# Batch 0 of a Longformer-attention and ResMLP kernel: the shifted V by compute engines, and a new order of batch 0's work

## The chip, the cores and the metric

The kernel runs on one core of a Trainium2 chip. The metric is device time in microseconds (us) of one execution. Engine names: PE is TensorE, PEld its weight loads, DVE VectorE, ACT ScalarE, POOL GpSimd, SP SyncE. "SPq" and the like are the engines' instruction queues, from which they issue transfers (DMAs).

## The reference

Eight batches of windowed attention with eight global tokens, followed by a residual MLP block that mixes tokens and then channels. Cut to what matters (B = 8, H = 8, S = 576, D = 64; the MLP width is 512, hidden 2048):

```
scores = scale * q @ k.T
mask = |i - j| <= 32, or i global, or j global
attn = softmax(where(mask, scores, -1e9))
x = (attn @ v), heads side by side: [B, S, 512]
a1 = alpha1 * x + beta1
u = x + lam * einsum('ts,bsd->btd', w_tok, a1)
a2 = alpha2 * u + beta2
out = u + lam * (relu(a2 @ w_ch1) @ w_ch2)
```

The eight global indices are data; the kernel reads them and gathers their K and Q rows.

## The kernel before

Attention is worked in 128-row tiles for pairs of heads (hp = 0..3, two heads a of 64 columns in 128 partitions). For a batch b, K and Q are transposed to KT and QP (in batch 0, Q0). Scores come by strips of 64 queries t against 128 keys, their exponentials go to E (ACT), the band mask is multiplied in to give PT (DVE, `probs_k`), and PGQ takes the part of the global keys (`probs_q`). The global queries' rows are scored by `gk0_mm`, exponentiated into EG and, with GM, become G (`g_rows`). `gq_mm` multiplies PGQ by V; its result goes to RG in a high part (`gq_hi`, ACT) and a low part (`gq_lo`, DVE). `pv_tiles` then adds up G with RG, PT with Ve and PT with Vo for five row tiles. Ve holds V in tiles of 128 rows that begin 32 rows early; Vo holds the same rows half a tile further down: its partitions 0 to 63 are partitions 64 to 127 of Ve's tile, and its partitions 64 to 127 are partitions 0 to 63 of Ve's next tile. After a normalisation (`norm_x` for tiles 0 to 2, `norm_y` or `norm_ya` for 3 and 4) comes the product with alpha1*lam (`scale_x`, `scale_y`, in LA1) into XL and XL4, which feed the token mixing with wtT.

The MLP of 4 row tiles at a time (`mlp`, nine groups g) is the large part: 64 matmuls of 128x512 with W1, whose results leave three PSUM banks through a ReLU on ACT to HT, and 64 with W2. While group g runs, the attention of batch g+1 is woven between its matmuls at fixed places (`weave`, `timed`). Batch 0 has no MLP to lie beside. Its work is written out by hand: FIRST is a list of words, each a function in `ops`, recorded in that order; each engine executes its own instructions in the order in which they were recorded. `name:b` gives a word PSUM bank b, and `sp:n` records n spare matmuls of 256 columns (`spare`), whose results nobody uses. The last words, W1s and after, begin the MLP of group 0 and the casts of batch 1.

The words that the text below uses, for hp = h: `ck`, `cq` cast K and Q to bf16; `tk`, `tq` transpose them on PE; `kt`, `qv` bring them from PSUM to KT and Q0; `gath`, `gx`, `gt`, `ge0`, `gte`, `ge1` gather and place the global columns; `ct`, `tt`, `ktt`, `qtt` do rows 512 to 575; `z` and `s` compute scores and `e` their exponentials; `V` and `u` load V of batch 0 and 1; `pg`, `pt` are the probabilities; `q`, `ra`, `rd` the global product and its two parts; `pvx`, `nx`, `xl` and `pvy`, `nr`, `ny`, `xm` the PV product, normalisation and scaling; `wt`, `we` transpose w_tok; `rs`, `re` its row sums; `la`, `lb`, `lc` spread alpha1*lam over LA1; `tm`, `ad`, `tx`, `ut` mix tokens, add, transpose and write UT, the MLP's input; `ab`, `abe` give the bias and scale columns of `ut`; `kc`, `qc` cast K and Q of batch 1. `beta` is the row b0_beta on POOL.

`ld_const` (word gat1) issues on SP the four transfers that fill Vo in batch 0, then K and Q of batch 1 and two broadcast rows. C16 is an index ramp of 576 f16 numbers, loaded from memory (L727) and used by `gm`. `fill_pt` puts zeros in the four PT buffers, `ve_fill` zeros and ones in Ve. CK, QV, QC and NY say, per hp, which engine does a step (A, D, P for ACT, DVE, POOL).

Of the kernel before, what the change touches and what calls it, by code (L numbers as in the profile page):

```python
# [9 lines left out]
FP32 = mybir.dt.float32  # L10
FP16 = mybir.dt.float16
# [5 lines left out]
P = 128  # L17
S = 576
D = 64
H = 8  # L20
HP = 4
# [22 lines left out]
]  # L44
FIRST = """
kgz vez ktz pgz gb1 gbm:0 W0 gbc ar0 ar1 gath ck0 ar2 pgc tk0:1 sp:3 cq0 kt0 ck1 tq0:2 V0 cq1 qv0 tk1:3 mask
V1 tq1:4 sp:6 kt1 qv1 ck2 V2 idn tk2:5 sp:2 cq2 V3 kt2 gx tq2:6 V4 ck3 qv2 gt:0 ge0 tk3:1 sp:3 gte wki ge1 kt3
cq3 gat1 wi z00:2 z20:3 s20:4 s00:5 e200 ct tq3:6 e000 GM z10:0 s10:1 tt:3 sp:7 e201 ptz e101 ktt qtt e001 qv3
ab:2 z21:4 z01:1 s01:3 fz e100 s21:5 gk0:6 e011 la e010 gk1:0 abe e210 pg0 z30:3 s30:1 e211 pt0 ptz2 z11:2
s11:4 eg0 q0:5 eg1 pg2 lb:6 b1t e110 G ra0 q2:0 e111 z31:2 sp:3 rd0 e300 pg1 s31:4 beta pvx0:5 pt1 e310 e311  # L50
q1:3 sp:2 e301 nx0 ra1 pvy0:2 qz0 wt0:4 ra2 rd1 rd2 lc wt4:1 pt2 wt3:5 we0 xl0 wt2:3 we3 nr0 ny0 pvy1:0 qz1
we2 wt1:6 nr1 pg3 pvx2:4 we1 pt3 xm0 q3:5 we4 nx2 pvy2:2 pvx1:3 ra3 v1f ny1 rd3 rs:6 nr2 ny2 xl2 xm1 pvy3:1 re
pvx3:4 xm2 nx1 tm0:5 xl1 u0 nx3 tm1:6 u1 ad0 u2 xl3 tx0:3 ad1 u3 tm2:4 ut0 nr3 ny3 u4 xm3 tx1:5 ad2 b1i tm3:6
ut1 gc1 tx2:3 ad3 ut2 tx3:4 ut3 W1s qc0 kc0 qc1 kc1 qc2 kc3 qc3 kc2
"""
PLACE = {t: (g, j) for g, ts in enumerate(GROUPS) for j, t in enumerate(ts)}


def _consts():
    p = np.arange(P)  # L60
    c16 = np.zeros((P, S), np.float16)
    c16[:, :] = np.arange(S)[None, :]
    d = p[:, None] - np.arange(64)[None, :]
    band = ((d >= 0) & (d <= 64)).astype(np.float16)
    eye = np.where(np.eye(P, dtype=bool), 0x3F80, 0).astype(np.uint16)
    ab = (p % 16) // 8
    oh = ((p >= 64) & (p < 80)) | ((p >= 96) & (p < 112))
    c32 = np.zeros((P, 144), np.float32)
    c32[:, 0:9] = 64 * np.arange(9)[None, :] - 32 + p[:, None]
    c32[:, 9:18] = (c32[:, 0:9] >= 0) & (c32[:, 0:9] < S)  # L70
    c32[:, 18:26] = p[:, None] % 8 == np.arange(8)[None, :]
    b2, h = p // 64, (p % 64) // 8
    for pr in range(4):
        c32[:, 26 + pr] = ((2 * pr + b2) * H + h) * S
    for a in range(2):
        c32[:, 30 + a] = h % 2 == a
        c32[:, 32 + a] = np.where(oh & (ab == a), GSC, 0.0)
        c32[:, 34 + a] = np.where((p < 64) & (ab == a), 1.0, np.where(p == 80, EPS_A, 0.0))
    c32[:, 36] = np.where(p < 64, 1.0, 1.0 / GSC)
    c32.view(np.uint16)[:, 96:224] = eye  # L80
    c32.view(np.uint16)[:, 224:288] = band.view(np.uint16)
    return c16, c32


def weave(mlp, parts):
# [15 lines left out]
def kernel(ctx, tc, q, k, v, global_idx, alpha1, beta1, w_tok, alpha2, beta2, w_ch1, w_ch2, lam, out):  # L101
    nc = tc.nc
# [8 lines left out]
    def T(name, shape, dt):  # L111
        return cp.tile(list(shape), dt, name=name)
# [14 lines left out]
    def mm(o, l, r, st, sp):  # L127
        nc.tensor.matmul(out=o, lhsT=l, rhs=r, start=st, stop=sp, skip_group_check=True)  # L128

    c16n, c32n = _consts()  # L130
    TSB = T("TSB", [P, DM], BF16)
    C16 = T("C16", c16n.shape, FP16)
    C32 = T("C32", c32n.shape, FP32)
    identb = C32[:, 48:112].bitcast(BF16)
    band = C32[:, 112:144].bitcast(FP16)
# [9 lines left out]
    Ve = [t.rearrange("p (c h e) -> p c h e", c=5, h=H) for t in Vef]  # L145
    Vo = [T(f"Vo{i}", [P, 4, H, 65], FP16) for i in range(2)]
# [5 lines left out]
    G = T("G", [P, 2, 704], FP16)  # L152
    GM = T("GM", [P, 2, S], FP16)
# [14 lines left out]
    mask = T("mask", [P, NW, 64], FP16)  # L168
# [3 lines left out]
    A2 = T("A2", [P, DM], FP32)  # L172
# [33 lines left out]
    TST = SR[:, 1, :]  # L206
# [221 lines left out]
        nc.vector.tensor_tensor(out=xo, in0=pv[:, :, :, 0:64], in1=rb, op=ALU.mult)  # L428

    def xl_eng(b, hp):  # L430
        return nc.vector if (b, hp) in ((0, 1), (0, 3)) else nc.gpsimd

    def pv_tiles(ps, b, hp, i0, i1):
        for i in range(i0, i1):
# [173 lines left out]
    def fill(ap, val=0.0, eng=None):  # L608
        (eng or nc.vector).memset(ap, val)
# [4 lines left out]
    def ld_kq(src, st_, eng, b, h0, h1):  # L614
        eng.dma_start(
            out=st_[:, h0:h1, :, :].rearrange("p h j d -> p h (j d)"), in_=src[b, h0:h1, 0:512, :].rearrange("h (p j) d -> p h (j d)", j=4)
        )
# [4 lines left out]
    def cast_q(b, hp, copy):  # L622
        copy(out=QB0[b][:, :, 128 * hp : 128 * hp + 128].rearrange("p j (a d) -> p a j d", a=2), in_=QST[:, 2 * hp : 2 * hp + 2, :, :])
# [95 lines left out]
    nc.sync.dma_start(out=gbi[0:1, :], in_=gi32.unsqueeze(0))  # L719
    nc.scalar.dma_start(out=C32[:, 0:48], in_=c32d[:, 0:48])  # L720
    nc.scalar.dma_start(out=C32[:, 48:144], in_=c32d[:, 48:144])
    for hp in range(HP):
        ld_kq(k, KST, nc.sync, 0, 2 * hp, 2 * hp + 2)
        ld_kq(q, QST, nc.scalar if hp < 2 else nc.sync, 0, 2 * hp, 2 * hp + 2)
    ld_tail(k, TST, nc.sync, 0, 0)
    ld_tail(q, TST, nc.sync, 0, 64)
    nc.sync.dma_start(out=C16, in_=nc.inline_tensor(c16n, name="c16_np").ap())  # L727
    nc.sync.dma_start(out=LA1[0:1, :], in_=alpha1.unsqueeze(0))
    for r in (0, 64):
        nc.sync.dma_start(out=LR[r : r + 1, :], in_=lam.unsqueeze(0))  # L730
# [21 lines left out]
    def ld_w2(blk):  # L752
        g_.dma_start(out=W2[:, 8 * blk : 8 * blk + 8, :], in_=w_ch2[1024 * blk : 1024 * blk + 1024, :].rearrange("(c p) e -> p c e", p=P))

    def fill_pt(i):
        z = PT0[i][:, 0, 0:64].bitcast(FP32)
        fill(bass.AP(z.tensor, z.offset, [z.ap[0], [608, 2], [64, 10], [1, 32]]), 0.0, g_)

    def pg_zero():
        for hp in range(HP):  # L760
# [3 lines left out]
    def ve_fill(i, eng=g_):  # L764
        fill(VF[i][0:32, 0:260], 0.0, eng)
        fill(VF[i][96:128, 1040:1300], 0.0, eng)
        fill(Ve[i][:, :, :, 64:65], 1.0, eng)
# [141 lines left out]
    def ab_ev(ps):  # L909
# [5 lines left out]
    mlp0 = mlp(0)  # L915
    hb = {}
    CPY = {"A": nc.scalar.copy, "D": nc.vector.tensor_copy, "P": nc.gpsimd.tensor_copy}
    CK, QV, KC, QC, NY = "ADAD", "ADAD", "AAAA", "DDDD", "DADD"
    ops = {
        "idn": lambda: nc.scalar.copy(out=ident, in_=identb),  # L920
        "kgz": kz_fill,
        "qz1": lambda: qzero(1, g_),
        "W0": warm,
        "ct": lambda: V_.tensor_copy(out=TSB, in_=TST),
        "gc1": lambda: gcols(1),
        "ktz": lambda: kt_fill(0, V_),
        "qz0": lambda: qzero(0, g_),
        "pgz": pg_zero,
        "vez": lambda: ve_fill(0, g_),
        "ptz": lambda: (fill_pt(0), fill_pt(1)),  # L930
        "ptz2": lambda: (fill_pt(2), fill_pt(3)),
        "gat1": ld_const,
        "wki": ld_wt,
        "wi": ld_w,
# [37 lines left out]
    for h in range(HP):  # L972
        ops.update(
            {
                f"ck{h}": lambda h=h: cast_k(h, CPY[CK[h]]),
                f"cq{h}": lambda h=h: cast_q(0, h, V_.tensor_copy),
                f"tk{h}": lambda ps, h=h: pair_tr(ps, KB0, h),
                f"tq{h}": lambda ps, h=h: pair_tr(ps, QB0[0], h),
                f"kt{h}": lambda h=h: pair_k(hb[f"tk{h}"], 0, h),
                f"qv{h}": lambda h=h: pair_q0(hb[f"tq{h}"], h, CPY[QV[h]]),  # L980
                f"V{h}": lambda h=h: load_v(0, h),
                f"u{h}": lambda h=h: load_v(1, h),
                f"kc{h}": lambda h=h: cast_k(h, CPY[KC[h]]),
                f"qc{h}": lambda h=h: cast_q(1, h, CPY[QC[h]]),
                f"pg{h}": lambda h=h: probs_q(0, h),
                f"pt{h}": lambda h=h: probs_k(0, h),
                f"q{h}": lambda ps, h=h: gq_mm(ps, 0, h),
                f"ra{h}": lambda h=h: gq_hi(hb[f"q{h}"], h),
                f"rd{h}": lambda h=h: gq_lo(hb[f"q{h}"], h),
                f"pvx{h}": lambda ps, h=h: pv_tiles(ps, 0, h, 0, 3),  # L990
                f"nx{h}": lambda h=h: norm_x(hb[f"pvx{h}"], 0, h),
                f"nr{h}": lambda h=h: hb.update({f"rt{h}": recip(hb[f"pvy{h}"], 2)}) if NY[h] == "A" else None,
                f"xl{h}": lambda h=h: scale_x(0, h),
                f"pvy{h}": lambda ps, h=h: pv_tiles(ps, 0, h, 3, 5),
                f"ny{h}": lambda h=h: norm_ya(hb[f"pvy{h}"], hb[f"rt{h}"], h) if NY[h] == "A" else norm_y(hb[f"pvy{h}"], 0, h),
                f"xm{h}": lambda h=h: scale_y(0, h),
                f"tm{h}": lambda ps, h=h: tok_mm(ps, h),
                f"ad{h}": lambda h=h: tok_add(hb[f"tm{h}"], h),
                f"tx{h}": lambda ps, h=h: tok_tr(ps, h),
                f"ut{h}": lambda h=h: tok_ev(hb[f"tx{h}"], h),  # L1000
            }
        )
# [142 lines left out]
```

## Time and profile before

| | |
|---|---|
| median of 9 runs | 394.21 us (392.98 to 396.75) |
| the profiled execution: time, span | 395.14 us, 393.4 us |
| PE, DVE, ACT, POOL busy | 96%, 58%, 43%, 53% of the span |
| transfers | 48.56 MB, mean 123 GB/s |
| first MLP matmul (W1s) | 43.82 us |
| first score matmul of batch 0 | 14.13 us |
| first PV matmul, and the one that waited for Vo | 23.27 us, 26.66 us |
| first ReLU of group 0 | 48.61 us |

The span runs from the first to the last instruction; the time has 1.74 us more around it. A line of the chain or of an engine's instructions gives start, duration and what it was (engine, source line, output<-input, shape, count), and in brackets how long the engine had been idle and for what. A line of the stretches gives, for each engine, busy time and number of instructions, then the granted clock of PE, the share of the transfer engines and GB/s. The busy shares of the page are means over the whole span, most of which is the MLP stream; what happens to batch 0 has to be read in the first 50 us.

### The profile page before, as it was taken

The page shows a single profiled execution, that of the slowest core. Times are in us where ns is not written, and L with a number is a line of the kernel's source. Part 1 is how long each engine was busy: PE and PEld are TensorE (multiplying, and loading weights), DVE is VectorE, ACT ScalarE, POOL GpSimd, SP SyncE. Part 2 cuts the span into 40 slices and gives each one's busy share as a digit, 9 for nine tenths or more (in the row PEclk, how much of TensorE's full clock was granted, in tenths as well). Part 3 has the DMA queues.
Part 4 walks back from the last instruction along what each step waited for, and adds up shares of the span by engine and source line. Part 5 has one row for each costly group of instructions (what it writes and reads, how often), then busy time and mean ns, then how long its engine had stood idle before and what let it go on. Part 6 is the DMA issues. An engine that isn't in the chain of part 4 may idle for free.

```text
span 393.4 us, 8133 instructions
## 1 busy us (share of the span) xinstructions
PE 376.0 (96%) x3062; PEld 213.0 (54%) x3115; DVE 228.8 (58%) x590; ACT 169.9 (43%) x335; POOL 209.1 (53%) x273
## 2 busy tenths in 40 slices
PE   6969899999999999999999999999999999999995
PEld 2649666645654566446645664466446644444443
DVE  5868765876548555954596459645774554114023
ACT  5544787005740584038503850187018700731720
POOL 8929819559748954885377836873251245000000
PEclk9977999999999999999999999999999999999999
DMA  7999999969999995999977998899240013101002
GB/s 239 184 236 292 162 215 150 127 149 124 159 147 147 142 153 122 104 122 168 151 77 153 129 147 103 130 168 129 78 108 27 2 55 80 41 20 61 28 27 81
DMA packets 161299, 48.56 MB, mean 123 GB/s; under 512 B 147615, under 2 KB 154727, under 8 KB 161260
## 3 DMA queue, kind: packets, MB, share of 16 engines
q0 software_dynamic: 98288, 17.05, 63.8%
q1 hardware_dynamic: 62140, 30.39, 37.7%
q10 hardware_dynamic: 832, 0.60, 0.5%
q8 instruction: 24, 0.39, 0.4%
q14 instruction: 15, 0.12, 0.1%
HBM read 39.05 MB, written 9.44 MB: 123 GB/s over the span
## 4 chain that ended last, share of the span: by engine, by line
PE 85%; DMA 6%; DVE 3%; POOL 3%; issue 1%; ACT 0%; DVEq 0%
PE bank L128 84%; DMA Ve<-in_v_dram 3%; DMA Vo<-Ve 2%; POOL Ve L222 2%; DVE XR L582 1%; DVE QP L644 1%; PE bank L869 1%; POOL KQG L254 1%; DVE OT L581 1%; PE bank L634 0%; POOL UB L507 0%; DMA gbi<-in_global_idx_dram 0%; DVE XR L428 0%; POOL XL L446 0%; DVE QP L238 0%
## 5 line engine op out<-in xcount | busy, mean ns | idle before, releaser
L128 PE MATMUL bank<-UT,W 128*128 128x512 bf16 x546 | 152.6, 379 | 1.1
L128 PE MATMUL bank<-W,HT 128*128 128x512 bf16 (+2 forms) x573 | 137.3, 373 | 0.9 <-issue 0.2
L566 ACT ACTIVATE HT<-bank,bias 128x512 bf16<-128x512 f32 x128 | 87.9, 687 | 52.3 <-PE bank L128 51.5
L367 ACT ACTIVATE E<-bank 128x416 f16<-128x416 f32 (+1 forms) x84 | 42.1, 520 | 116.3 <-PE bank L128 115.5
L128 PEld LDWEIGHTS <-HT 128*128 128x128 bf16 (+1 forms) x610 | 55.1, 99 | 53.9 <-issue 1.6
L446 POOL TENSOR_TENSOR XL<-XR,LA 128x384 bf16<-128x384 f32 x30 | 30.3, 1011 | 79.6 <-DVE XR L428 49.2
L128 PEld LDWEIGHTS <-W 128*128 128x128 bf16 (+1 forms) x658 | 51.4, 97 | 25.5
L581 DVE TENSOR_TENSOR OT<-bank,LAM 128x512 f32<-128x512 f32 (+2 forms) x37 | 24.9, 673 | 55.2 <-PE bank L128 55.1
L507 POOL TENSOR_TENSOR UB<-XR,A 128x512 bf16<-128x512 f32 x28 | 35.9, 1290 | 22.5 <-DVE XR L502 15.1
L128 PE MATMUL bank<-RG,G 128*128 128x65 f16 x320 | 45.0, 197 | 0.3
L128 PE MATMUL bank<-Ve,PT 128*128 128x65 f16 x300 | 42.5, 197 | 0.0
L128 PEld LDWEIGHTS <-PT 128*128 128x128 f16 x540 | 32.0, 99 | 17.7 <-DMA Vo<-Ve 1.0
L128 PE MATMUL bank<-XL,wtT 128*128 128x512 bf16 (+2 forms) x237 | 41.0, 326 | 0.1
L128 PEld LDWEIGHTS <-G 128*128 128x128 f16 x320 | 31.8, 100 | 16.8 <-issue 1.8
L128 PE MATMUL bank<-Vo,PT 128*128 128x65 f16 x240 | 34.3, 194 | 2.8 <-DMA Vo<-Ve 2.8
L222 POOL DMA_DIRECT2D Ve<-in_v_dram x40 | 34.4, 882 | 0.2
L128 PEld LDWEIGHTS <-KT 128*128 128x128 bf16 (+1 forms) x324 | 23.2, 100 | 18.0 <-issue 1.4
L215 POOL DMA_DIRECT2D Kb<-in_k_dram x30 | 27.2, 907 | 5.0 <-DMA W<-in_moe_w_ch_dram 4.9
L128 PE MATMUL bank<-QP,KT 128*128 128x144 bf16 (+1 forms) x252 | 28.7, 223 | 0.4
L215 POOL DMA_DIRECT2D Qb<-in_q_dram x30 | 27.1, 904 | 3.6 <-DMA W<-in_moe_w_ch_dram 3.6
L428 DVE TENSOR_TENSOR XR<-bank,rd 128x384 f32<-128x384 f32 (+1 forms) x63 | 26.9, 426 | 2.4 <-DVE rd L421 0.3
L128 PEld LDWEIGHTS <-wtT 128*128 128x128 bf16 (+1 forms) x240 | 18.7, 99 | 17.4 <-issue 1.7
(153 smaller groups left out, 416.0 us busy)
## 6 DMA issues: line engine op xcount, KB each, us to landing
out_dram<-XR SPq DMA_DIRECT2D x31, 256.0 KB, 4.1
W<-in_moe_w_ch_dram POOLq DMA_DIRECT2D x4, 1024.0 KB, 16.3
Vo<-Ve SPq DMA_DIRECT2D x14, 260.0 KB, 3.8
Ve<-in_v_dram POOLq DMA_DIRECT2D x24, 128.0 KB, 5.5
Kb<-in_k_dram POOLq DMA_DIRECT2D x24, 128.0 KB, 6.3
Qb<-in_q_dram POOLq DMA_DIRECT2D x24, 128.0 KB, 6.3
Ve<-in_v_dram POOLq DMA_DIRECT2D x16, 96.0 KB, 6.7
XR<-in_k_dram SPq DMA_DIRECT2D x4, 256.0 KB, 4.3
```

The lines of the kernel that those rows point to most:

```text
L128: nc.tensor.matmul(out=o, lhsT=l, rhs=r, start=st, stop=sp, skip_group_check=True)
L215: nc.gpsimd.dma_start(out=dst[0:n, c, :].rearrange("p (h d) -> p h d", d=D), in_=src[b, :, c * P : c * P + n, :].rearrange("h p d -> p h d"))
L222: nc.gpsimd.dma_start(out=Ve[b % 2][r0 : r0 + hi - lo, c, :, 0:D], in_=v[b, :, lo:hi, :].rearrange("h p d -> p h d"))
L254: nc.gpsimd.indirect_dma_start(out=g, out_offset=None, in_=src, in_offset=bass.IndirectOffsetOnAxis(ap=hidx[:, pr : pr + 1], axis=0))
L367: nc.scalar.activation(out=eb(b, hp)[:, UOFF[u] : UOFF[u + 1]], in_=ps[:, 0:n], func=AF.Exp, bias=0.0, scale=0.125)
L428: nc.vector.tensor_tensor(out=xo, in0=pv[:, :, :, 0:64], in1=rb, op=ALU.mult)
L446: xl_eng(b, hp).tensor_tensor(out=XL[b % 2][:, 0:3, cs], in0=XR[:, base : base + 3, cs], in1=lb, op=ALU.mult)
L507: nc.gpsimd.tensor_tensor(out=ub, in0=x, in1=A2, op=ALU.mult)
L566: nc.scalar.activation(out=HT[:, ec, :], in_=st[ec], func=AF.Relu, bias=b_, scale=1.0)
L581: nc.vector.tensor_tensor(out=ot, in0=ps, in1=LAM[:, lo:hi], op=ALU.mult)
L582: nc.vector.tensor_tensor(out=x, in0=ot, in1=x, op=ALU.add)
L644: nc.vector.tensor_copy(out=QP[r, hp, a, 0:8, 0:64].rearrange("p t (u j) -> p t u j", j=4), in_=ps[r, 0:512].rearrange("p (j t u) -> p t u ...
```

## The change

Only batch 0's part and the constants change.

- Vo of batch 0 is filled by four copies: va1 (DVE, 64 partitions x 1560 elements), vb1 (POOL, the same size), va2 and vb2 (DVE, 64 x 520). The four SP transfers go. In their place `ld_const` issues one transfer of 4 bytes from Ve to A2, which is overwritten later.
- C16 is made by an iota on POOL (word io); its transfer goes, and K and Q of batch 0 are issued in another order, with one of K on ACT's queue.
- Zero fills: Ve's move from POOL to DVE; of PT's four, one stays on POOL and three are copies of a zero on ACT.
- The engines of several steps change: CK "ADAD" to "AAAD", QV "ADAD" to "ADDD", QC "DDDD" to "AAAA", NY "DADD" to "AADA", `ct` from DVE to ACT, and `scale_x`, `scale_y` of hp 1 from DVE to POOL.
- FIRST has a new order. Its spare matmuls are 31 instead of 26, 16 of them in a row behind tq0; hp 2 is worked first in PV; mask and GM come early; u0 to u3 come ahead of xl2, ut0 behind abe.

```
 FIRST = """
-kgz vez ktz pgz gb1 gbm:0 W0 gbc ar0 ar1 gath ck0 ar2 pgc tk0:1 sp:3 cq0 kt0 ck1 tq0:2 V0 cq1 qv0 tk1:3 mask
-V1 tq1:4 sp:6 kt1 qv1 ck2 V2 idn tk2:5 sp:2 cq2 V3 kt2 gx tq2:6 V4 ck3 qv2 gt:0 ge0 tk3:1 sp:3 gte wki ge1 kt3
-cq3 gat1 wi z00:2 z20:3 s20:4 s00:5 e200 ct tq3:6 e000 GM z10:0 s10:1 tt:3 sp:7 e201 ptz e101 ktt qtt e001 qv3
-ab:2 z21:4 z01:1 s01:3 fz e100 s21:5 gk0:6 e011 la e010 gk1:0 abe e210 pg0 z30:3 s30:1 e211 pt0 ptz2 z11:2
-s11:4 eg0 q0:5 eg1 pg2 lb:6 b1t e110 G ra0 q2:0 e111 z31:2 sp:3 rd0 e300 pg1 s31:4 beta pvx0:5 pt1 e310 e311
-q1:3 sp:2 e301 nx0 ra1 pvy0:2 qz0 wt0:4 ra2 rd1 rd2 lc wt4:1 pt2 wt3:5 we0 xl0 wt2:3 we3 nr0 ny0 pvy1:0 qz1
-we2 wt1:6 nr1 pg3 pvx2:4 we1 pt3 xm0 q3:5 we4 nx2 pvy2:2 pvx1:3 ra3 v1f ny1 rd3 rs:6 nr2 ny2 xl2 xm1 pvy3:1 re
-pvx3:4 xm2 nx1 tm0:5 xl1 u0 nx3 tm1:6 u1 ad0 u2 xl3 tx0:3 ad1 u3 tm2:4 ut0 nr3 ny3 u4 xm3 tx1:5 ad2 b1i tm3:6
-ut1 gc1 tx2:3 ad3 ut2 tx3:4 ut3 W1s qc0 kc0 qc1 kc1 qc2 kc3 qc3 kc2
+kgz vez io ktz pgz gb1 gbm:0 W0 gbc ar0 pz1 ar1 gath ck0 ar2 pgc tk0:1 sp:3 cq0 mask idn tq0:2 sp:16 V0 pz3 GM
+qv0 V1 pz2 cq1 V2 tq1:3 kt0 cq2 V3 tq2:4 sp:1 ck2 qv1 qv2 ck1 tk2:5 V4 kt2 ck3 tk1:6 wki cq3 gat1 kt1 tk3:0 wi
+kt3 gx tq3:2 ct qv3 gt:1 tt:3 sp:3 ge0 gte fz ktt ge1 qtt z20:4 s20:5 gk1:6 e201 la e200 z21:0 z11:2 s11:1
+gk0:3 b1t eg1 va1 s21:5 e111 z00:4 s00:6 eg0 z10:1 sp:2 va2 e210 s10:3 vb1 G e211 z01:0 sp:2 e001 s01:5 e100
+lb:6 e011 pz0 e010 pg2 z31:1 s31:5 lc v1f pt2 ab:0 sp:2 e310 q2:6 e000 u0 wt1:1 ra2 wt3:4 sp:2 we1 pg0 u1 rd2
+pvx2:6 e101 vb2 pt0 e311 u2 pvy2:1 e110 q0:3 nx2 we3 wt0:5 u3 pg1 ra0 wt2:2 nr2 ny2 we0 wt4:6 xl2 rd0 we2 q1:4
+pt1 z30:1 s30:5 pvx0:3 we4 xm2 pvy0:2 nx0 ra1 rs:6 e300 beta rd1 e301 nr0 pg3 pvy1:1 re pvx1:3 ny0 pt3 xl0
+q3:4 tm2:5 ra3 nr1 ny1 rd3 xm0 nx1 pvy3:6 pvx3:2 ad2 xl1 tm0:4 nx3 xm1 nr3 ad0 ny3 tx2:3 u4 tm1:5 xl3 b1i xm3
+tx0:4 ad1 tm3:6 abe ut0 qz0 ut2 tx1:5 ad3 qz1 ut1 tx3:4 gc1 ut3 W1s qc1 kc1 qc0 kc0 qc3 kc2 kc3 qc2
 """
...
-        return nc.vector if (b, hp) in ((0, 1), (0, 3)) else nc.gpsimd
+        return nc.vector if (b, hp) in ((0, 3),) else nc.gpsimd
...
-    for hp in range(HP):
-        ld_kq(k, KST, nc.sync, 0, 2 * hp, 2 * hp + 2)
-        ld_kq(q, QST, nc.scalar if hp < 2 else nc.sync, 0, 2 * hp, 2 * hp + 2)
+    for eng, x, h in ((0, k, 0), (1, q, 0), (0, k, 1), (1, k, 2), (0, q, 1), (0, q, 2), (0, k, 3), (0, q, 3)):
+        ld_kq(x, KST if x is k else QST, (nc.sync, nc.scalar)[eng], 0, 2 * h, 2 * h + 2)
...
-    nc.sync.dma_start(out=C16, in_=nc.inline_tensor(c16n, name="c16_np").ap())
...
     def ld_const():
-        ve, vo = Ve[0], Vo[0]
-        for c in (0, 2):
-            nc.sync.dma_start(out=vo[0:64, c : c + 2], in_=ve[64:128, c : c + 2])
-            nc.sync.dma_start(out=vo[64:128, c : c + 2], in_=ve[0:64, c + 1 : c + 3])
+        nc.sync.dma_start(out=A2[0:1, 0:1], in_=Ve[0][0:1, 3, 0, 0:2].bitcast(FP32))
...
-    def fill_pt(i):
+    def fill_pt(i, eng):
         z = PT0[i][:, 0, 0:64].bitcast(FP32)
-        fill(bass.AP(z.tensor, z.offset, [z.ap[0], [608, 2], [64, 10], [1, 32]]), 0.0, g_)
+        z = bass.AP(z.tensor, z.offset, [z.ap[0], [608, 2], [64, 10], [1, 32]])
+        if eng is nc.scalar:
+            eng.copy(out=z, in_=bass.AP(zero.tensor, zero.offset, [zero.ap[0], [0, 2], [0, 10], [0, 32]]))
+        else:
+            fill(z, 0.0, eng)
...
-    CK, QV, KC, QC, NY = "ADAD", "ADAD", "AAAA", "DDDD", "DADD"
+    CK, QV, KC, QC, NY, PZ = "AAAD", "ADDD", "AAAA", "AAAA", "AADA", "PAAA"
...
-        "ct": lambda: V_.tensor_copy(out=TSB, in_=TST),
+        "ct": lambda: nc.scalar.copy(out=TSB, in_=TST),
...
-        "vez": lambda: ve_fill(0, g_),
-        "ptz": lambda: (fill_pt(0), fill_pt(1)),
-        "ptz2": lambda: (fill_pt(2), fill_pt(3)),
+        "vez": lambda: ve_fill(0, V_),
+        "io": lambda: g_.iota(out=C16, pattern=[[1, S]], base=0, channel_multiplier=0, allow_small_or_imprecise_dtypes=True),
+        "va1": lambda: CPY["D"](out=Vo[0][0:64, 0:3], in_=Ve[0][64:128, 0:3]),
+        "vb1": lambda: CPY["P"](out=Vo[0][64:128, 0:3], in_=Ve[0][0:64, 1:4]),
+        "va2": lambda: CPY["D"](out=Vo[0][0:64, 3], in_=Ve[0][64:128, 3]),
+        "vb2": lambda: V_.tensor_copy(out=Vo[0][64:128, 3], in_=Ve[0][0:64, 4]),
```

More of the change, by code (lines that the diff above doesn't have):

```diff
@@ L60, in _consts @@
     p = np.arange(P)
-    c16 = np.zeros((P, S), np.float16)
-    c16[:, :] = np.arange(S)[None, :]
     d = p[:, None] - np.arange(64)[None, :]
@@ L81, in _consts @@
     c32.view(np.uint16)[:, 224:288] = band.view(np.uint16)
-    return c16, c32
+    return c32
 def weave(mlp, parts):
@@ L128, in mm @@
         nc.tensor.matmul(out=o, lhsT=l, rhs=r, start=st, stop=sp, skip_group_check=True)
-    c16n, c32n = _consts()
+    c32n = _consts()
     TSB = T("TSB", [P, DM], BF16)
-    C16 = T("C16", c16n.shape, FP16)
+    C16 = T("C16", [P, S], FP16)
     C32 = T("C32", c32n.shape, FP32)
@@ L984 @@
                 f"qc{h}": lambda h=h: cast_q(1, h, CPY[QC[h]]),
+                f"pz{h}": lambda h=h: fill_pt(h, (g_, V_, nc.scalar)["PDA".index(PZ[h])]),
                 f"pg{h}": lambda h=h: probs_q(0, h),
```

## The prediction

> **What bounds the kernel now.** I read the chain that ended last, then the engine stretches of five microseconds, then each engine's instructions in order of time up to 62 us. Columns of the first are start, duration, what.
>
> ```profile
> 6.17 3.88 POOL Ve L222 x4
> 10.05 7.36 DMA Ve<-in_v_dram
> 17.43 9.19 DMA Vo<-Ve
> 26.66 1.90 PE bank L128 x21
> ...
> 43.82 1.89 PE bank L128 x8
> ```
>
> From 43.82 us on (W1s, the first MLP matmuls) nearly every piece is TensorE at L128, so 349.6 of the 393.4 us are the MLP stream, which the change leaves alone; what can move is how early it begins. Ahead of it 20.4 us of the chain are V: it is loaded by 17.4, then copied half a tile down (Ve to Vo) by four transfers on SP, the last landing 9.19 us after its issue because W1 fills the DMA engines. TensorE stands:
>
> ```profile
> 23.68 0.19 PE L128 MATMUL bank<-Ve,PT 128*128 128x65 f16 x1
> 26.66 0.21 PE L128 MATMUL bank<-Vo,PT 128*128 128x65 f16 x1 [2.79 <-DMA Vo<-Ve]
> ```
>
> and pays a second time through its clock (the column after the five busy times):
>
> ```profile
> 20.00:25.00 5.00, 3.15 (x49) 1.89 (x42) 3.83 (x12) 2.83 (x9) 1.86 (x2) 0.99 1.07 242
> 25.00:30.00 5.00, 3.34 (x39) 2.95 (x39) 2.70 (x6) 1.74 (x4) 1.14 (x2) 0.50 1.07 230
> 30.00:35.00 5.00, 5.00 (x78) 4.78 (x76) 4.24 (x17) 3.51 (x9) 4.37 (x10) 0.50 1.24 258
> 35.00:40.00 5.00, 4.95 (x86) 4.46 (x86) 4.19 (x10) 0.89 (x2) 5.00 (x8) 0.99 1.32 320
> ```
>
> Half clock from 24.9 to 35.1: the 65-column matmuls take 243 ns there, 192 ns after it, and their starts are 0.055 us apart instead of 0.03. That is 2.8 us of stall and up to 4 us of slow PE. Before 18 us PE is slow too (four bf16 transposes take 0.61 us there, 0.39 at 45.8), although the row reads 1.00.
>
> **The change, part by part** (starts by the trace of before; new places by adding its durations along each engine's compiled order).
>
> *V.* Four SP transfers become four copies. va1 (64x1560 f16) and the 520-column va2, vb2 go on DVE, vb1 (64x1560) on POOL. No row shows a DVE f16 copy; nearest are the f32 cast of 512 in 0.42 us (1560 at that rate: 1.2 us) and, as a floor, half of it. I take 0.9 for va1, 0.3 each for the others. For POOL the ends are a memset (64x1296 in 1.17 us, so 1.4 us) and a two-input product (128x384 in 1.00 us, so 4.1 us); one input is nearer the memset: 2.0.
>
> *POOL's queue.* Fills of Ve leave it (0.77), the index ramp enters it (576 elements: 0.5 by the memset, 1.5 by the product; 0.8), so the PGQ fills end at 3.6 as before; the gathers wait for DVE, which has Ve's fills in front (+0.35): gathers to 6.5, V issues to 11.2, W loads 2.3 to 13.4. Three probability fills are gone from here, so the other fills (2.25) end at 15.7, the TSB loads at 17.1, vb1 at 19.1. V must be there: V4 had landed by 17.4. Then one fill 0.75, batch 1's V fills 1.4, four V loads 3.5 (they were behind the XL products): 24.7. XL for hp 2, beta, hp 0 and hp 1 (1.0+0.95 each, 1.3 for beta; hp 1 was DVE's 1.1) wait in turn for their normalisations: hp 2 done 26.6, beta 27.9, hp 0 29.9, hp 1 32.2.
>
> *The front.* DVE gets mask, EG and GM (0.75+0.38+1.4) ahead of the second Q cast, which so goes from 8.3 to about 9.2; one K cast and the TSB cast move to ACT, one Q eviction to DVE. ACT gets three zero fills; its 512-element cast takes 0.62 and 128 elements 0.30, so 640 elements cost 0.73, the first directly ahead of the first K cast (4.26 to 4.95). On PE 16 spare matmuls of 0.21 us stand between the first and second Q transpose, 7.3 to 10.7, while the casts are awaited. Behind them DVE's order counts: two Q evictions of 0.69 (to 12.5), the last K and Q casts (13.4), the gathered rows 0.6 (14.0); so transposes end at 14.8. The global columns go DVE, ACT, DVE as before (1.3 us from 14.6): first scores at 15.95 (14.13 before). So the front is 1.8 us later. K, Q loads are in another order on the two queues but the same bytes, and the 147 KB ramp is gone.
>
> *Scores to the first PV.* Seven score units of 0.24 us (1.7), global scores 0.96, the alpha row 0.85, two w_tok transposes 0.5, eight spares 0.86 and one global-row product 0.27 are 5.1 us of PE at full clock; the exponentials (0.35 apart) keep pace. PV of hp 2 starts at 22.1, with Vo complete at 19.1 (last piece: vb2 on DVE at 22.4, ready for the second bank). Before: 26.66.
>
> *PV to W1s.* DVE's remaining list, each at its start-to-start cost (product with mask 0.82, PGQ 0.54, x rows 0.8, y rows 0.7, lo rows 0.3, reciprocals 0.2, four adds of 0.65, one hp's XL 1.05, small casts 0.25), sums to 13.1 us: 35.2 if never waiting. Two y normalisations go from DVE to ACT. POOL's hp 1 at 32.2 lets tm1 (1.1) run to 33.3 and its add to 34.2; then tm3, its add 35.65, the transposes 0.5: W1s at 36.2 against 43.82.
>
> *What is late next.* ut0 waits for the bias columns, moved behind ad1, so the four UT evictions run to 37.25. Behind them ACT has eight casts of 0.54, where before it had four (2.17 us) with DVE doing the Q half: to 41.5, then three KT copies, and the first ReLU:
>
> ```profile
> 44.48 2.17 ACT L620 CAST UT<-XR 128x512 bf16<-128x512 f32 x4
> ...
> 48.61 0.60 ACT L566 ACTIVATE HT<-bank 128x512 bf16<-128x512 f32 x1
> ```
>
> It comes at 43.0 against 48.61. PE can't run ahead, as its three MLP banks wait for it. So 7.6 us at W1s become **5.6 us** at the ReLU. Batch 1's K and Q on SP begin at 17 instead of 18, behind one dummy transfer that waits for V3; without 0.53 MB of Vo in front they land near 37, where the casts want them, but share the engines with batch 1's V, now issued 13 us earlier. W2 moves from 39.9 to 34; its landing took 16 us and it is used some 27 us after W1s, so it is covered.
>
> *Where a rule speaks against the change: the clock.* The row: PE was busy 3.41 of 3.41 us in 28.3 to 31.7 and stayed at 0.50; it had dropped after a stretch (21.5 to 24.9) that was 2.40 of 3.41 busy. The Trainium skill, "TensorE: Matmul & The Clock Gate", Part 1, says about 3.4 us of sustained activity give full clock and an idle window takes it. By the page alone the 16 spares (3.4 us) would warm PE once and it would stay so: 5.6 us. By the rows, PE has only about 2 of 4.7 us of work between 11.3 and 16, less than the stretch that dropped it, so scores are likely to start at half clock again. One window of 3.4 us at half clock costs 1.7 us; I take that. Ends: 0, and 5.1 (three windows, as in the trace).
>
> *And POOL's first library call.* The compiled order has a library reload in front of the ramp; before, the same reload stood in front of L863:
>
> ```profile
> 18.59 0.70 POOL L626 DMA_DIRECT2D TSB<-in_q_dram  x1
> 19.43 1.31 POOL L863 TENSOR_TENSOR XL<-UB 1x512 bf16<-1x512 f32 x1
> ```
>
> 0.14 us of gap, and 2.6 ns an element as in L446: nothing. The skill's "GPSIMD Engine Reference", 2.1 Instruction dispatch, prices a first call to freshly loaded code at about 6 us. I take the row, 0, and keep 6.
>
> *DVE and POOL together.* The same 512-element cast took 0.42 beside V descriptor issue and 1.61 at 11.28 us beside W1's:
>
> ```profile
> 10.02 0.42 DVE L623 CAST Kb<-XR 128x512 bf16<-128x512 f32 x1
> ...
> 11.28 1.61 DVE L620 CAST UT<-XR 128x512 bf16<-128x512 f32 x1
> ```
>
> One or two such hits in the new order are 1.2 us each; they widen the range.
>
> **Sum.** 5.6 - 1.7 = 3.9 us. The profiled execution took 395.14 (span 393.4 and 1.74 around it), 0.93 above the median 394.21. Its own time would become 391.2; a median, **390.3 us**. A measurement of this kernel can tell about 0.3% (1.2 us) from no change: below 393.0 is faster, above 395.4 slower.
>
> **Rivals.**
> (A) Forecast, 0.50: V no longer waits, PE cold for about one window; DVE, POOL and ACT set the end. Own range 387.5 to 392.7.
> (B) Clock holds from the spares on, 0.20: the full 5.6 us, 388.6. For: 18.1 to 21.5 was 2.69 busy and held. Against: the thin stretch before 16.
> (C) Half clock through the whole stage, 0.16; this one ends slower. PE work from 15.95 to W1s is 16.7 us at full clock in a plan of 20.2, so 3.5 us of slack; time c at half clock costs c/2 - 3.5. From c = 18.2 us the 5.6 are gone. If PE is held cold until the dense W1s, c is 24 or more: 8.5 us of cost, 394.2 - 5.6 + 8.5 = 397.1. For: small matmuls took three windows to wake it. Against: they did wake it after 10.2.
> (D) POOL's reload costs 6 us, 0.06: everything behind the ramp is 5.5 us later: 395.8.
> (E) The pieces don't come sooner, 0.08: vb1 at 4.1 us or locked out by DVE moves POOL's chain 2.1 us one for one: 392.4. The same holds if the casts find batch 1's loads still in flight.
>
> **Numbers.** A gives 0.47 faster, B 0.20, E 0.06: 0.73, less 0.01 for unlisted mishaps. C and D give 0.19 slower, with 0.01 from those. The rest, 0.08, is no change. Range 387.0 (B with cheap copies) to 396.5 (most of C and D).
>
> **What would show it.** No DMA Vo<-Ve in batch 0; no wait of PE on V near 22 to 27; first PV at 22 to 24 and W1s at 36 to 38. Step by step: vb1 near 2 us ending by 20; POOL's ramp under 1 us and the gathers issued near 4; XL hp 1 on POOL at 32; first ReLU at 43 to 45, with ACT's casts in front. The granted clock after 11 us tells A from B and C. Wrong if first scores come after 18, if PE waits for POOL copies at 20 to 25, if POOL starts the gathers near 10 (D), or if the first ReLU is no earlier than 48.6.

## The result, and the profile after

The changed kernel took 389.58 us (median of 10 runs, 389.25 to 393.1) against 394.65 us for the kernel before beside it: ratio 0.9891, 95% interval 0.9868 to 0.9913. Two later comparisons of the same two kernels gave 0.9883 (0.9852 to 0.9914) and 0.9915 (0.9887 to 0.9943). The forecast was 390.3 us and faster. The first profiled execution of the changed kernel took 391.28 us with a span of 389.5 us.

The chain that ended last, of the changed kernel (start, duration, what):

```profile
1.15 2.96 DMA C<-c_np
4.12 8.26 DMA XR<-in_q_dram
...
15.37 5.52 PE bank L126 x67
...
31.82 7.60 DMA LAM<-in_moe_lam_dram
...
39.47 0.61 ACT OT L621
```

V is gone from it: no Ve, no Vo. In its place the front hangs on Q of batch 0, which lands at 12.4 us. At the end of the stage the chain names batch 1's transfers on SP, whose last row (LAM) lands at 39.4; but ACT went from the UT evictions into batch 1's casts (L621 and L618) without a gap, so that landing and ACT's own row of work come out level there. The same markers as before (first scores, first PV, W1s, first ReLU), in the PE and ACT instructions of the changed kernel:

```profile
15.06 0.74 PE L126 MATMUL bank<-W,KT 64*128 64x72 bf16 x10
...
22.87 0.19 PE L126 MATMUL bank<-RG,G 128*128 128x65 f16 x1
...
38.89 1.89 PE L126 MATMUL bank<-UT,W 128*128 128x512 bf16 x8
...
45.15 0.60 ACT L564 ACTIVATE HT<-bank 128x512 bf16<-128x512 f32 x1
```

First PV starts at 22.87 and no instruction of it waits for V (before: 23.27, stopped until 26.66). W1s comes 4.9 us sooner, the first ReLU 3.5 us sooner, and the span is 3.9 us shorter; the 0.4 us by which it gains more than the ReLU are not traced. The stretches of five microseconds (busy PE, PEld, DVE, ACT, POOL, then the granted clock):

```profile
15.00:20.00 5.00, 4.93 (x68) 2.69 (x68) 3.32 (x6) 3.45 (x11) 3.54 (x7) 0.68 1.48 193
20.00:25.00 5.00, 4.71 (x77) 3.36 (x77) 4.13 (x14) 4.52 (x13) 4.89 (x10) 1.00 1.06 219
25.00:30.00 5.00, 4.20 (x81) 3.07 (x81) 4.74 (x15) 3.79 (x11) 4.66 (x7) 1.00 1.08 232
...
40.00:45.00 5.00, 2.93 (x29) 1.75 (x28) 1.87 (x4) 4.80 (x11) 3.62 (x6) 1.00 2.05 175
```

The half clock of 24.9 to 35.1 has gone; one window of 3.41 us is left, at 14.75 to 18.16, under the first scores. (Below, "a window" is such a stretch of 3.41 us at half clock.) DVE, not PE, is the fullest engine from 25 to 30 us, and ACT from 40 to 45, where it works through the eight casts in front of the ReLU.

### The profile page after: what moved, and what is told of

Same layout as the page of the kernel before. It is cut to its first block, busy times and chain, and to the rows that moved or that the text cites. A ratio compares the mean times of both kernels' runs of the same rounds, so it can differ in the third digit from the quotient of the medians.

```text
span 389.5 us, 8144 instructions
## 1 busy us (share of the span) xinstructions
PE 372.5 (96%) x3067; PEld 208.7 (54%) x3120; DVE 227.9 (59%) x584; ACT 175.5 (45%) x351; POOL 210.0 (54%) x272
## 4 chain that ended last, share of the span: by engine, by line
PE 87%; DMA 5%; DVE 4%; ACT 2%; issue 1%; SPq 1%; ACTq 0%; DVEq 0%
PE bank L126 87%; DMA XR<-in_q_dram 2%; DMA LAM<-in_moe_lam_dram 2%; DMA C<-c_np 1%; ACT OT L621 1%; DVE PT L330 1%; DVE XR L426 1%; ACT UT L618 0%; DVE XR L580 0%; DVE OT L579 0%; SPq L737 0%; DVE QP L642 0%; PE bank L632 0%; SPq L613 0%; DVE RG L387 0%
## 5 line engine op out<-in xcount | busy, mean ns | idle before, releaser
L444 POOL TENSOR_TENSOR XL<-XR,LA 128x384 bf16<-128x384 f32 x31 | 31.2, 1007 | 71.8 <-DVE XR L426 49.8
L579 DVE TENSOR_TENSOR OT<-bank,LAM 128x512 f32<-128x512 f32 (+2 forms) x37 | 24.9, 674 | 55.2 <-PE bank L126 55.0
L126 PE MATMUL bank<-RG,G 128*128 128x65 f16 x320 | 43.1, 193 | 0.7 <-DVE RG L387 0.4
L126 PE MATMUL bank<-Ve,PT 128*128 128x65 f16 x300 | 41.1, 194 | 0.0
L126 PEld LDWEIGHTS <-PT 128*128 128x128 f16 x540 | 30.9, 98 | 16.5
L126 PEld LDWEIGHTS <-G 128*128 128x128 f16 x320 | 30.7, 97 | 15.9 <-DVE RG L387 0.9
L126 PE MATMUL bank<-Vo,PT 128*128 128x65 f16 x240 | 33.3, 192 | 0.0
L580 DVE TENSOR_TENSOR XR<-OT,XR 128x512 f32<-128x512 f32 (+2 forms) x33 | 27.4, 829 | 1.6
```

What stands on the lines that cost most here:

```text
L444: xl_eng(b, hp).tensor_tensor(out=XL[b % 2][:, 0:3, cs], in0=XR[:, base : base + 3, cs], in1=lb, op=ALU.mult)
L579: nc.vector.tensor_tensor(out=ot, in0=ps, in1=LAM[:, lo:hi], op=ALU.mult)
L580: nc.vector.tensor_tensor(out=x, in0=ot, in1=x, op=ALU.add)
```

## The experiments

"Theory 1" below says that V's transfers, and the half clock behind the stall, were the bound; "theory 2" that the gain is the new order's. "The new order" stands for all of the change but V: FIRST, the engines, the fills, the ramp and the order of the loads. Ratios are to the kernel before, run beside it.

**One half of the change at a time.** First the new order with V still by transfer:

```
-        nc.sync.dma_start(out=A2[0:1, 0:1], in_=Ve[0][0:1, 3, 0, 0:2].bitcast(FP32))
+        (the four transfers Ve to Vo of before)
 FIRST: words va1, va2, vb1, vb2 taken out
```

> The changed kernel with the four transfers Ve to Vo put back on SP (at the same word, gat1) and the four copies and the 4-byte transfer taken out; the new order stays. Theory 1 (V's transfers were the bound, and the half clock behind the stall a part of it): the last piece lands near 26 us again, behind W1's data; TensorE stands 2 to 4 us ahead of the first PV matmuls that read Vo, the clock drops, W1s comes at 42 to 44 instead of 38.9, and the time is 393 to 395.5 (1.0 to 1.5% over the changed kernel). Theory 2 (the gain is the new order: transposes with spares, early masks, work shared out): V's transfers are hidden or cost little, 389.5 to 391.

Measured: 394.8 us, ratio 1.0035 (1.0019 to 1.005). Its PE instructions:

```profile
22.74 0.20 PE L126 MATMUL bank<-Vo,HT 128*128 128x65 f16 x1 [1.34 <-DMA Vo<-Ve]
...
26.15 0.23 PE L126 MATMUL bank<-Vo,HT 128*128 128x65 f16 x1 [2.88 <-DMA Vo<-Ve]
```

PE reaches V sooner and stands longer (4.2 us), then runs at half clock again, from 24.2 to 31.0; W1s is at 41.55, the ReLU at 48.10. The new order by itself gains nothing, and is 0.35% slower. The other half, the old order with V by copies:

```
+ ops va1, va2, vb1, vb2; the 4-byte transfer in ld_const in place of the four
 FIRST of before: va1 ahead of e210, va2 vb2 behind pt0, vb1 ahead of b1t
```

> The kernel before, with only V's part of the change: va1 ahead of pg0, va2 and vb2 behind pt0 on DVE, vb1 ahead of b1t on POOL, and the 4-byte transfer in place of the four. Theory 1: the copies put 1.2 us on DVE ahead of the first PV, which starts near 24.5 and does not stall; the clock stays full; W1s near 39.5 to 41, time 390 to 392 (0.7 to 1.1% under the kernel before). Theory 2: DVE becomes the bound at once, and no more than 1.5 us is left: 393 or more.

Measured: 393.03 us, ratio 0.9978 (0.9962 to 0.9994). The wait for Vo is gone, W1s is at 41.41, and the ReLU, at 46.42, is 2.2 us sooner than before. But PE now stands earlier, for the transfer of the alpha row, and DVE's products are slow:

```profile
19.30 0.20 PE L904 MATMUL bank<-ident,abr 8*128 8x8 f32 x1 [2.71 <-DMA abr<-in_moe_alpha_dram]
```

```profile
20.06 0.56 DVE L929 COPY Vo<-Ve 64x1560 f16<-64x1560 f16 x1
...
20.86 1.89 DVE L332 TENSOR_TENSOR PT<-E,mask 128x640 f16<-128x640 f16 x2
22.78 0.96 DVE L931 COPY Vo<-Ve 64x520 f16<-64x520 f16 x1
23.77 0.29 DVE L932 COPY Vo<-Ve 64x520 f16<-64x520 f16 x1
```

The same copy of 64x520 takes 0.96 us beside POOL's work and 0.29 us without it, and DVE is busy 4.86 us of the five from 20 to 25 (3.83 before). Was it the 2.71 us, then, that hid V's gain? The same kernel with the alpha transposes moved away:

```
-ab:2 z21:4 ... gk1:0 abe va1
+z21:4 ... gk1:0 va1 ...  lb:6 vb1 b1t ab:2 abe e110
```

> The kernel before with V by the four compute copies (as in the run of V alone), and with the alpha transposes, for which TensorE stood 2.71 us there until 19.30, moved behind the lambda product. Theory 1 (V alone would have given the gain, and that stall hid it): first PV at 23 to 24, W1s about 39.5, ReLU 44.5, time 390.5 to 391.5. Theory 2 (in the old order VectorE, busy nearly throughout 14 to 41 with GpSimd reading beside it, sets the end): the stall goes, W1s stays at 41 to 41.5 and the time at 392.5 to 393.2.

Measured: 393.46 us, ratio 0.997 (0.9953 to 0.9987), in the time no better than with that wait. PE now stands for DVE, which is busy 4.91 of the five us from 20 to 25, on products slowed beside POOL:

```profile
25.71 0.70 PE L128 MATMUL bank<-Ve,PGQ 128*128 128x130 f16 x5 [1.99 <-DVE PGQ L325]
```

The profiles don't compare the two cleanly: this one took 394.39 us, its clock first came to full at 20.94 us and was half from 24.4 to 31.2, and W1s at 44.04 and the ReLU at 48.82 are later than either theory had them.

By the times, V alone is worth 0.2 to 0.3%, the order alone nothing, and both together 0.9 to 1.2%: the old order, with the copies where these two runs put them, has no room on DVE for them, and the new one has no use until V comes early. That is theory 1 for the cause, theory 2 for what the old order permits. Other places for the copies in the old order were not tried, and these runs do not separate the stall for V from the half clock behind it; the sorting by clock below bears on that.

**The spare matmuls and the clock.** Fifteen of the sixteen spares taken out:

```
-tq0:2 sp:16 V0
+tq0:2 sp:1 V0
```

> The changed kernel with 1 spare matmul behind tq0 instead of 16. Theory 1 (the spares buy full clock early): TensorE is then cold from the start until the scores have filled a window, 18 to 22 us; scores and global scores (5 us of matmuls at full clock) take up to twice that, first PV 1.5 to 3 us later, time 391 to 392.5. Rival (TensorE has slack there, the exponentials and DVE set the pace): under 0.5 us, 389.3 to 390.0.

Measured: 391.2 us, ratio 0.9928 (0.9905 to 0.9951), beside 0.9883 to 0.9915 for the changed kernel. PE's clock first comes to full at 19.3 us in its trace (7.92 with the spares), and stays. The rows of the stretches read 1.00 before that too; the durations show the difference. The same four transposes with 1 spare, then with 16:

```profile
13.95 0.61 PE L667 MATMUL bank<-C,TSB 128*128 128x128 bf16 x4
```

```profile
14.28 0.40 PE L667 MATMUL bank<-C,TSB 128*128 128x128 bf16 x4 [0.68 <-ACT TSB L921]
```

W1s at 38.87 and the ReLU at 45.43 match the changed kernel's execution that had a window. By the traces, then, these spares are worth about what one window costs; in time the two intervals overlap. Then the opposite, more spares between 11 and 15 us:

```
-V2 tq1:3 kt0 / ck3 tk1:6 wki / kt1 tk3:0 wi / qv3 gt:1 tt:3
+V2 tq1:3 sp:6 kt0 / ck3 tk1:6 sp:6 wki / kt1 tk3:0 sp:3 wi / qv3 gt:1 sp:6 tt:3
```

> The changed kernel with 21 more spare matmuls, in four places between 11 and 15 us. Theory clock: the half-clock window behind the first scores goes, the granted clock stays 1.00 from about 8 us on, and a profiled run is 1.0 to 1.7 us shorter than one of the changed kernel that has the window (about 389.5 to 389.9 against 391.3); where the changed kernel has no window, it gains nothing. Rival (DVE sets the end, PE has slack in this stage): first ReLU stays within 0.5 us of 45.15 and the time within 0.5 us of the changed kernel's. If the spares stand in the way of transposes, first scores come later than 15.5 and it is slower.

> The changed kernel once more, so that the next three stand beside it on one chip. 389.2 to 390.5 us, ratio to before 0.987 to 0.992. Whether the second half-clock window (14.7 to 18.2 us) is in its profile is what decides between about 389.4 and about 391.

Measured: 390.13 us against 390.35 us for the changed kernel on the same chip, so nothing in the median. The profiled execution did hold its clock: first the changed kernel's row, then this one's.

```profile
15.00:20.00 5.00, 5.00 (x69) 2.66 (x68) 3.35 (x6) 3.50 (x11) 3.47 (x6) 0.69 1.69 174
```

```profile
15.00:20.00 5.00, 4.74 (x77) 2.65 (x77) 4.41 (x10) 4.13 (x13) 3.85 (x6) 1.00 1.30 186
```

It has W1s at 36.97 and the ReLU at 43.23, with a span of 387.6 us against 389.3. So the window costs what it was thought to cost, 1.7 us there, but these spares don't decide whether one comes. One window lowers an execution's mean granted clock by 0.0044; a little more is lost at half clock at the end of some, so 0.998 and above is counted as no window, 0.994 to 0.996 as one. By this count 5 of its 11 executions had none, and 11 of 24 of the changed kernel. Sorted so, the executions of the changed kernel have a median of 389.37 us without a window (11) and 390.87 us with one (8), and lie at 391.67 to 393.55 us with more (5). The kernel before had a window in 89 of the 91 executions that ran beside these kernels, three in the middle case; it took 392.78 us in the two without and 393.74 us in the 35 with about three. By these figures the clock is the smaller part of the gain: with no window on either side, 392.78 against 389.37 us, 3.4 us of it are left. The first of them rests on two executions only.

**DVE beside POOL.** The scaling of head pair 0 on DVE, so that POOL does not read beside pg3 and pt3:

```
-        return nc.vector if (b, hp) in ((0, 3),) else nc.gpsimd
+        return nc.vector if (b, hp) in ((0, 0), (0, 3)) else nc.gpsimd
```

> The changed kernel with the XL products of head pair 0 on VectorE in place of GpSimd, so that GpSimd does not read beside VectorE from 28.9 to 30.8. Theory contention: pg3 falls from 1.27 to about 0.55 us and pt3 from 1.11 to about 0.82, 1.7 us less for the four products, against 1.1 us that XL adds on VectorE: first ReLU 0 to 0.6 us earlier, time within 0.5 us of the changed kernel. Rival (no contention, the products are slow by their place): pg3 stays near 1.2 us, VectorE's list is 1.1 us longer, and the ReLU and the time are 1 us later.

Measured: 389.48 us, ratio 0.9854 (0.9829 to 0.9879), beside 390.35 us. pg3 on DVE in the changed kernel, and what POOL does then; after them, pg3 in this one:

```profile
28.94 1.00 POOL L444 TENSOR_TENSOR XL<-XR,LA 128x384 bf16<-128x384 f32 x1
...
29.14 1.27 DVE L323 TENSOR_TENSOR PGQ<-W,gqm 128x80 f16<-128x80 f16 x2
```

```profile
27.39 0.31 DVE L323 TENSOR_TENSOR PGQ<-W,gqm 128x80 f16<-128x80 f16 x2
```

The disturbance is real: 0.31 against 1.27 us for the same two products, and 0.82 against 1.11 for pt3 behind them. It is also no loss that this edit can recover: DVE's own scaling takes as much, W1s is at 36.94 and the ReLU at 43.20 (its window came later, at 42.7 to 46.1), and the executions without a window have a median of 389.31 us, as the changed kernel's 389.37. The lower median comes with fewer windows in five executions.

**ACT's casts in front of the ReLU.** Batch 1's Q casts on DVE, as before the change:

```
-    CK, QV, KC, QC, NY, PZ = "AAAD", "ADDD", "AAAA", "AAAA", "AADA", "PAAA"
+    CK, QV, KC, QC, NY, PZ = "AAAD", "ADDD", "AAAA", "DDDD", "AADA", "PAAA"
```

> The changed kernel with the casts of batch 1's Q back on DVE (QC DDDD), nothing else. Theory 1 (ACT's eight casts, 39.5 to 44.2, are what delays the first ReLU and give back 1.5 us of the 4.9 at W1s): KT copies start near 41.6 instead of 43.6, first ReLU at 43.2 to 44 instead of 45.15, time 388.0 to 388.8. Rival (DVE's own copies of Q, or batch 1's data still in flight, set the pace): first ReLU within 0.4 us of 45.15, time 389.2 to 390.2.

Measured: 388.95 us, ratio 0.9877 (0.9849 to 0.9904). In an execution without a window W1s is at 36.85, and the ReLU:

```profile
42.11 0.60 ACT L564 ACTIVATE HT<-bank 128x512 bf16<-128x512 f32 x1
```

This is 1.1 us before the 43.2 of the two profiles above (more spares; scaling on DVE) that also kept full clock up to W1s. By the trace the eight casts on ACT were a cost of the change. In time the executions without a window differ by 0.6 us (388.74 against 389.37), but these ran on different chips, on which the median of the kernel before differed by up to 1.1 us, and the ratios overlap: the gain in time is not settled. Going on along that row, the bias columns ahead of ad1 (`abe`), two UT evictions early, and the global columns of batch 1 on ACT in its idle 1.65 us:

```
-nr3 ad0 ny3 tx2:3 u4 ... ad1 tm3:6 abe ut0 qz0 ut2 tx1:5 ad3 qz1 ut1 tx3:4 gc1 ut3 W1s
+nr3 ad0 abe ny3 tx2:3 ut2 u4 ... ut0 ad1 gc1 tm3:6 qz0 tx1:5 ad3 qz1 ut1 tx3:4 ut3 W1s
-        "gc1": lambda: gcols(1),
+        "gc1": lambda: gcols(1, nc.scalar.copy),
```

> The changed kernel again, to stand beside the two built on it. 389.2 to 390.5 us, ratio to before 0.987 to 0.992; first ReLU about 45.2 us if the profiled run has the half-clock window at 14.7 to 18.2, about 43.3 if it has none.

> Batch 1's Q casts on VectorE as before the change, the bias columns ahead of ad1 so that two of the four UT evictions run in ScalarE's idle 1.65 us, and batch 1's global columns on ScalarE there too. Theory (ScalarE's row of work between W1s and the first ReLU sets the end, then VectorE's): W1s stays at 36.9 (38.9 with a half-clock window), ScalarE starts its four casts 1.4 us sooner, VectorE's Q copies 1.9 us sooner, first ReLU at 40.2 to 41.0 without a window, 1.1 to 1.9 us before that of the run with the Q casts alone (42.11); time 387.2 to 388.0 us. Rival (the batch 1 loads of K and Q, or the MLP's later stages, set the end): ReLU as before or the time unchanged at 388.9.

Measured: 389.75 us, ratio 0.9906 (0.9874 to 0.9937), against 390.31 us and 0.9915 for the changed kernel on the same chip. Theory had 387.2 to 388.0: a miss, though three of the six executions had three windows or more, and the three without have a median of 388.27. The ReLU came at 41.40 us, 0.7 sooner than with the Q casts alone instead of 1.1 to 1.9, for the time gained on DVE went to POOL's fills beside its casts:

```profile
35.22 2.57 POOL L608 MEMSET QP<- 64x1296 f32 x2 [0.31 <-ACT QP L249]
...
35.69 3.06 DVE L622 CAST OT<-XR 128x512 bf16<-128x512 f32 x4
```

The run with the Q casts alone has those four casts in 1.66 us. And the 0.7 us is lost further on. At DVE's second output product (L579; here L580) this kernel is 1.27 us ahead of the run with the Q casts alone (72.02 against 73.29 us), at the fifth 0.28 us behind (111.46 against 111.18). In between PE meets a wait:

```profile
86.37 0.59 PE L126 MATMUL bank<-UT,W 128*128 128x512 bf16 x2 [1.64 <-DMA UT<-UB]
```

These are the first W1 matmuls of the MLP's second group, whose input the transposing transfers UT<-UB write from batch 1's results; the run with the Q casts alone does not wait there. It is not only that PE has caught up: here SP issues the five transfers from 78.74 us, there from 77.67, and why they are later is not traced. With head pair 0's scaling on DVE as well:

> The same, and head pair 0's XL products on VectorE in place of GpSimd. By the run that made this change alone it is worth nothing in itself (W1s 36.94 against 36.97 and 36.85 in the runs without a half-clock window); expected within 0.5 us of the kernel without it. A gain of more than 0.5 us would say that GpSimd's reads beside VectorE cost more than the one pair of products shows.

Measured: 389.14 us, ratio 0.9878 (0.9857 to 0.9899), with the ReLU at 42.35 behind a window at 21 to 25, and 0.97 us of the same wait at 86.75. The median is 0.6 us under the run before it, but without a window the two are alike, 388.28 and 388.27 us (3 executions each), as expected. Last, the two QP fills on ACT:

```
-        "qz1": lambda: qzero(1, g_),   "qz0": lambda: qzero(0, g_),
+        "qz1": lambda: qzero(1, nc.scalar),   "qz0": lambda: qzero(0, nc.scalar),
-nr1 ny1 rd3 ... tm3:6 qz0 tx1:5 ad3 qz1 ut1
+nr1 ny1 qz0 qz1 rd3 ... tm3:6 tx1:5 ad3 ut1
```

> The kernel before this one (Q casts on VectorE, early bias columns, global columns on ScalarE, XL of head pair 0 on VectorE) with the two zero fills of QP, GpSimd's 2.57 us that ran beside VectorE's four Q casts, made by ScalarE copies in its idle 2.35 us ahead of the last y normalisation. Theory (VectorE's casts took 3.06 us in place of 1.66 because GpSimd's fills ran beside them, and VectorE then holds TensorE's transposes and the first ReLU): the casts fall to 1.7 us, the interval from W1s to the first ReLU from 5.0 to about 3.7 to 4.3 us, time 387.5 to 388.6, 0.6 to 1.3 us less. Rival: the casts run as long beside the DMA issues that GpSimd now does there (V, W2, gathers), the interval stays near 5.0 and the time near 389.1; or the two fills delay the last y normalisation on ScalarE and W1s by as much as the casts gain.

Measured: 388.64 us (388.15 to 388.80 in all six executions), ratio 0.9837 (0.9808 to 0.9867), the lowest of all. The interval from W1s (37.62) to the ReLU (42.62) still is 5.0 us, as the rival had it, but for another reason, which DVE shows:

```profile
36.92 0.86 DVE L622 CAST OT<-XR 128x512 bf16<-128x512 f32 x2
38.52 0.76 DVE L622 CAST OT<-XR 128x512 bf16<-128x512 f32 x2 [0.74 <-DMA XR<-in_q_dram]
```

The casts fell to 1.6 us, and the second pair then waited for batch 1's Q to land. No execution had more than one window. Without a window the median is 388.44 us (4 executions), against 388.28 us (3) in the run above, on another chip, so the fills are not shown to have gained anything. It is the version with the lowest ratio to the kernel before; its interval lies below that of the changed kernel's first comparison (0.9868 to 0.9913) and overlaps another (0.9852 to 0.9914). The ratio flatters it: beside it the kernel before took 394.82 us, its highest median here. None of its times is above 388.80 us, and of the changed kernel's 24 one is below that (388.49). How much of this is that no execution had more than one window, and whether that would last, six executions don't tell.

## Why the prediction was right, point by point

- *The bound.* Right: V's arrival and the half clock behind it. The two half-changes show that it was a necessary cause, and not sufficient. The prediction did not say that the copies needed the new order to pay, and it gave the half clock up to 4 us; the kernel before took only 1.0 us less without a window (two executions) than with three.
- *The front, 1.8 us later.* Mis-sized: 0.9 us (15.06 against 14.13). The last Q cast ended at 12.83 instead of 13.4; it waited 0.23 us for its transfer, so DVE's list was shorter than it was costed and Q's landing at 12.4 us sets the front.
- *Scores to the first PV.* The 5.1 us of PE work listed lead from 15.95 to 21.05; the 22.1 of the forecast holds 1.05 us more, for which no term is named. Measured without a window, in the run with the Q casts: 15.16, where nine of the first ten score matmuls start, to 21.54, 6.4 us. So more than the listed work stands there.
- *The copies.* vb1 1.50 us (forecast 2.0), va1 0.58 (0.9), va2 0.29 (0.3), vb2 0.70 (0.3). The floor given for DVE was the better neighbour where POOL did not disturb. vb1 ended at 19.83 instead of 19.1: it waited for V itself.

```profile
0.86 0.60 POOL L927 IOTA C<- 128x576 f16 x1 [0.40 <-POOLq L1130]
...
18.33 1.50 POOL L929 COPY Vo<-Ve 64x1560 f16<-64x1560 f16 x1 [1.40 <-DMA Ve<-in_v_dram]
...
32.77 1.00 POOL L444 TENSOR_TENSOR XL<-XR,LA 128x384 bf16<-128x384 f32 x1 [2.01 <-DVE XR L426]
```

- *The ramp.* 0.60 us, with 0.40 us idle in front of it (0.29 before POOL's first fill in the kernel before), gathers at 4.08: rival D fell, and the row of before was right against the 6 us of the Trainium skill's "GPSIMD Engine Reference", 2.1 Instruction dispatch.
- *POOL's chain.* hp 1 came at 32.77 to 34.6 (forecast done by 32.2), behind DVE and not behind its own work; without a window, in the run with the Q casts, 31.03 to 32.85.
- *PV to W1s.* Forecast 36.2, from DVE's list never waiting. Measured 38.89 with the window, 36.85 to 36.97 in the profiles with full clock up to there. The list was right to 0.7 us.
- *Contention.* Taken as range only, and mis-sized: beside POOL's work DVE took 1.76 us for G (0.81 before), 0.70 for vb2 (0.29 elsewhere), 1.32 for pt1 (0.82), 1.27 for pg3 (0.31) and 1.11 for pt3 (0.82), 3.1 us in all on the fullest engine. W1s without a window missed by 0.7 us only, for the front was 0.9 us shorter and va1 0.3 us cheaper than costed; the rest of the difference is not traced. Errors met here, and that W1s came so near is in part luck.
- *What is late next.* UT evictions, eight casts, KT copies on ACT: as forecast. The ReLU without a window is at 43.2 (forecast 43.0), with it at 45.15 (43.0 and 1.7). Gain at the ReLU 5.4 us or 3.5 us, against 5.6 and 3.9. Moving four casts away made it 1.1 us earlier. Batch 1's Q was to land near 37; in the last run DVE stood for it until 38.5.
- *The clock term.* The place and length were right in three profiles of three of this kernel (one window, from 14.7 to 15.0 on), and 1.7 us agrees with 1.5 by the sorted executions and with 1.7 by the two profiles on one chip. The rule of the Trainium skill's "TensorE: Matmul & The Clock Gate", Part 1, by which PE would stay warm from the spares on, held in 11 of 24 executions; one window, the reading from the rows, came in 8. (The mean clock doesn't say where the window lay.) So A and B were about equally frequent, and the chances of 0.50 and 0.20 leaned too much on one profile. C, half clock throughout, didn't occur in any profile. Its formula, c/2 - 3.5, would make one window free, against the 1.7 us charged in A; the measured 1.5 to 1.7 us show that PE's 3.5 us of slack do not lie where the window does.
- *The sum.* 5.6 - 1.7 = 3.9 us; the profiled span fell by 3.9 us. The median of all 24 executions is 390.35 us, the forecast 390.3. So close an agreement is luck: that median lies between executions without a window and with one, and the ReLU itself gained 3.5 us.

## What to carry to other kernels

Taking away a stall pays only as far as the next engine has room: try each half of a change alone before you put the gain down to one of them. In a stage where PE has slack, write down the cost of a half-clock window as a term of its own and sort executions by granted clock before comparing medians; otherwise a difference of one window passes for a gain or hides one. When a stage at the head of a long stream has been shortened, look for the first transfer that the stream then has to wait for.

## What the hardware showed that was not expected

- The granted clock changes in the records at multiples of 3.41 us within an execution (its states are 3.41, 6.83, 10.24 or 13.65 us long, or longer), but the first full clock comes at another moment in each: 7.92 us in the changed kernel, 9.12 us with the Q casts moved, though the program up to there is the same. Over the fixed five microseconds from 10 to 15, PE busy 3.00 us kept the clock in one execution (the early evictions) and 3.13 lost it in another (the changed kernel, third comparison). Cut instead at the clock's own windows of 3.41 us, counted from the first full clock, the second window sorts this stretch: PE was busy 1.69, 1.91 and 2.01 us in the three profiles of the changed kernel, which then lost the clock, and 2.11 to 2.36 us in the runs with V by transfer, the Q casts moved, head pair 0's scaling on DVE, the early evictions, and the two runs with both of the last, which kept it. Busy time alone is still not the rule: the kernel before lost its clock behind a window that was 2.40 us busy, and the run with the early evictions and DVE's scaling behind one of 3.01.
- A DVE operation beside POOL is stretched by very unequal amounts: a copy of 64x520 f16 from 0.29 to 0.96 us (1.57 beside vb1 in the run with head pair 0's scaling on DVE), two products of 128x80 from 0.31 to 1.27, four casts of 128x512 from 1.66 (1.42 before) to 3.06 beside a memset. POOL pays too: its 128x384 product took 1.35 us instead of 1.00 in the run with early evictions.
- A POOL f16 copy of 64x1560 takes 1.50 us (1.48 to 1.82 over all runs), where a POOL two-input product of 128x384 takes 1.00: about 1 and 2.6 ns an element.
